# Segmented attention with a gated feed-forward block on one core: order of the first loads, warm-up operand, output buffers and the written order

## The chip, the cores and the metric

The kernel runs on one core of a Trainium2 chip. The metric is the device time of one execution in microseconds (us). TensorE (PE in the profile) multiplies matrices into PSUM, VectorE (DVE), ScalarE (ACT) and GpSimd (POOL) work on tiles, SyncE (SP) issues most DMAs and ScalarE some. Each engine runs its own instructions in the order in which they were written, and waits for the others on semaphores.

## The reference

All inputs are bf16. `x` is 2048 x 512; it is cut into 4 segments of 512 rows. Two branches read the same `x`, and a gate per row mixes them.

```
g   = sigmoid((x * gate_w).sum(-1))                      # one number a row
# branch a: 32 heads of width 16, 4 segments of 512 rows, in order
q, k, v = x @ wq, x @ wk, x @ wv
for s in range(4):
    a_dot = softmax(causal(q_s k_s^T / 4)) v_s
    a_mem = phi(q_s) M / (phi(q_s) z + 1e-6)             # phi(t) = t + 1 if t > 0 else exp(t)
    o_s   = sigmoid(beta) * a_mem + (1 - sigmoid(beta)) * a_dot
    M, z  = M + phi(k_s)^T v_s, z + phi(k_s).sum(rows)
a   = o @ wo
# branch b: feed-forward, width 1792
b   = (relu(x @ W_gate) * (x @ W_up)) @ W_down
out = g * a + (1 - g) * b
```

## The kernel before

The four segments are worked on one after another, and overlap. For a segment, TensorE projects q, k and v (`proj_q`, `proj_k`, `proj_v`), and for each group `c` of 8 heads it makes scores (`qk`, `qk_diag`), which ScalarE turns into exponentials `E` and `Em` (`score`), GpSimd and VectorE mask, and TensorE multiplies with the values (`pv`). VectorE divides by the row sums and turns the result into `oT` (`normalise`). From the second segment on, `dens` and `recall` add the memory's part by way of two DMAs through HBM (`coefs`, then `cdr`). `ffn_tasks` makes 14 feature tiles: a gate product, ScalarE's rectifier into `rgr`, an up product, and VectorE's product of both into `hT`. `out_tile` then adds `hT` times `wd_sb` and `oT` times `wo_sb` in one PSUM bank for 128 output rows. VectorE scales them by the row's factor (`ngcol`, L851) into a buffer of the ring `osr`, and SyncE stores that (L854). The ring has two buffers. The last 128 rows (tile 15) are made in two halves of 256 columns.

Matmuls come in three forms: whole (L442, all 128 x 128 of the array), cut into four strips of 32 columns (L446; also `pv`, `dens`, `memory`), and cut into four strips of 32 rows (the scores, L600 and L613). A projection, feed-forward or output matmul (a "flex" task) is issued whole or as four strips, according to what stands before it on TensorE.

**The order of the work is a written list.** Each piece of work is a `Task`, made by `plan.add` with an engine, a planned duration, the tasks it depends on, and the buffers it needs and frees. Tasks are numbered in the order of these calls. `ORDER` lists all 1337 numbers; `Plan.run` takes the tasks in that order, and each engine gets its instructions in it. `UNITS` gives, one hexadecimal digit a buffer, which buffer of its ring (or which of the 8 PSUM banks, `ps`) each piece of work uses. The planned durations and the landing times `LANDS` (in ns) don't act when the kernel runs; they are what the list was made from.

**The opening.** Loads are issued in program order. The first segment's `x` comes as four tiles of 128 rows into `xn` (names n0 to n3), and TensorE turns them with an identity matrix (`x0_tasks`, L478), VectorE and ScalarE copying the results to `xT` (L486; tile 1 and the second half of tile 3 on ScalarE). `wq` comes in two row halves (`load_q`), `wk` and `wv` whole. SyncE issues n0, the first half of wq, n3, the second half, wk, wv, then the gate and up weights in pieces; ScalarE issues n1 and n2. The first segment's q projection is split so that each half of `wq`, and the first two x tiles, can be used as they arrive (`proj_q`, `seg == 0`). Until the first tile is there, TensorE runs 6 matmuls on a tile of zeros (`heat`, L866), which VectorE sets first (`junk`, L312). Two more such matmuls of 256 columns (L493) are tasks of their own behind the turning of tiles 1 and 2; the list puts one of them there and the other, number 33, in the middle of the kernel.

Of the kernel before, what the change touches and what calls it, by code (L numbers as in the profile page):

```python
# [92 lines left out]
"""  # L93

UNITS = (
    "3527401612502452222115110640030222230110000031010000001001000000100100000320000137310d122a"
    "5222100c12292011023401083010111631250013103b1110000130311102301022221231212020224120112000"
    "0023001031000012001110000002300120320000120113137102a31122001020d1238123b01001035002920130"
    "106303c30240011110030201320210131200012021023332101062000002301112000003401012000000230111"
    "02100002301020320219211a203402200018120571271136302b320c21110233603d0000111130312130003112"  # L100
    "220312002002100000200111200000300110500000001011111000024000302032323029112b71332235714c21"
    "37720d3104602850665231522a1010010110"
)


class Slot:


    def __init__(self, cands):
        self.cands, self.units, self.left = tuple(cands), (), 0  # L110

    @property
# [66 lines left out]
def kernel(  # L179
# [64 lines left out]
    omr = ring([P, L], BF16, "omr", 3)  # L244
    dnr = ring([P, P], F32, "dnr", 2)
    cdr = ring([P, L], F32, "cdr", 2)
    osr = ring([P, D], BF16, "osr", 2)
    plan.pool("ps", 8)
    ps = psum.tile([P, 8 * L], F32, name="ps")

# [42 lines left out]
    def load_q(i):  # L293
        return load(nc.sync, wq_sb[:, 2 * i:2 * i + 2, :],
                    A_wq.rearrange("(c p) n -> p c n", p=P)[:, 2 * i:2 * i + 2, :], "q" + "ab"[i])
# [635 lines left out]
```

## Time and profile before

| what | value |
|---|---|
| median of 3 runs | 266.69 us (266.48, 266.69, 267.89) |
| profiled execution, its own time | 267.34 us |
| its span, first to last instruction | 265.5 us |
| busy in the span: PE, DVE, ACT, POOL | 260.6, 203.0, 183.0, 62.3 us |
| first matmul; first x tile turned; first q projection | 1.06, 3.59, 5.33 us |
| landings of n0, n1, first wq half, n2, n3, second wq half | 3.47, 3.64, 4.83, 4.87, 5.21, 5.92 us |
| landings of wk, wv, first gate piece, first up piece | 9.23, 10.74, 12.26, 13.74 us |
| last matmul ends; last scaling begins; last store lands | 261.69, 262.51, 264.56 us |
| DMA traffic | 19.43 MB, 73 GB/s in the mean, 340 to 380 GB/s from 3 to 14 us |

Times in the profile count from the first instruction. A line of the timeline has the start, the duration, the engine, the source line, the operation, the tiles written and read, the count, and in brackets how long the engine had been idle before and what ended that. Consecutive instructions of a kind are merged in it, and a matmul's end is modelled, so the distance between starts is the surer measure. PEld is the loading of a matmul's stationary operand. A landing is the last of the 16 parts into which a DMA is split.

### The profile page before, as it was taken

What the parts mean: (1) busy time and instruction counts of PE and PEld (TensorE: products, weight loads), DVE (VectorE), ACT (ScalarE), POOL (GpSimd) and SP (SyncE); (2) the same over time, 40 slices, a digit from 0 to 9 for tenths busy, and PEclk for the clock granted to TensorE, in tenths of its full rate; (3) what the DMA queues carried; (4) which work ended last, traced back from release to release, by engine and by line L of the source; (5) the groups of instructions that cost most, each with busy time, mean ns of one, the idle gap of its engine ahead of it and who ended that gap; (6) DMA issues with size and microseconds to landing.
All of it is one profiled execution on the core that took longest, in us unless ns stands there. A gap on an engine that the chain in (4) does not pass through costs nothing.

```text
span 265.5 us, 8410 instructions
## 1 busy us (share of the span) xinstructions
PE 260.6 (98%) x3646; PEld 120.2 (45%) x3646; DVE 203.0 (76%) x455; ACT 183.0 (69%) x168; POOL 62.3 (23%) x162
## 2 busy tenths in 40 slices
PE   8999999999999999999999999999999999999994
PEld 4543444453435444444443444444443544444553
DVE  3499698879897979899988988987882675476631
ACT  3098898979797798889889666889576663932000
POOL 7001914134114123141405140304004050210000
PEclk9999999999999999999999999999999999999999
DMA  6999916120002247610004231000300100300011
GB/s 222 347 217 345 295 37 87 34 71 2 2 30 46 91 75 116 165 32 2 2 12 62 81 85 49 16 2 1 129 6 0 42 0 7 124 3 0 2 42 42
DMA packets 29884, 19.43 MB, mean 73 GB/s; under 512 B 14872, under 2 KB 28312, under 8 KB 29848
## 3 DMA queue, kind: packets, MB, share of 16 engines
q1 hardware_dynamic: 29560, 18.64, 27.7%
q8 instruction: 28, 0.46, 0.8%
q10 hardware_dynamic: 288, 0.26, 0.3%
q14 instruction: 8, 0.07, 0.1%
HBM read 13.21 MB, written 2.55 MB: 59 GB/s over the span
## 4 chain that ended last, share of the span: by engine, by line
PE 95%; DMA 3%; DVE 0%; ACTq 0%; issue 0%; DVEq 0%
PE ps L442 63%; PE ps L446 14%; PE ps L600 8%; PE ps L673 7%; DMA out_dram<-osr 1%; DMA xn<-in_A_x_dram 1%; PE ps L613 1%; PE ps L778 1%; DVE osr L851 0%; PE ps L478 0%; PE ps L729 0%; ACTq L266 0%; PE ps L493 0%; DVEq L851 0%
## 5 line engine op out<-in xcount | busy, mean ns | idle before, releaser
L622 ACT ACTIVATE E<-ps 128x2048 bf16<-128x2048 f32 x64 | 120.1, 1877 | 31.9 <-PE ps L600 29.7
L651 POOL TENSOR_SCALAR_AFFINE_SELECT E<-E 128x256 bf16<-128x256 bf16 x128 | 53.5, 453 | 150.1 <-ACT E L622 150.0
L442 PE MATMUL ps<-xT,wu_sb 128*128 128x512 bf16 x200 | 54.4, 380 | 0.0
L829 DVE TENSOR_TENSOR hT<-ps,rgr 128x512 bf16<-128x512 f32 x56 | 38.2, 684 | 19.9 <-PE ps L442 14.2
L442 PE MATMUL ps<-xT,wg_sb 128*128 128x512 bf16 x188 | 49.5, 380 | 0.0
L823 ACT ACTIVATE rgr<-ps 128x512 bf16<-128x512 f32 x56 | 32.5, 596 | 15.5 <-PE ps L442 14.8
L442 PE MATMUL ps<-wd_sb,hT 128*128 128x512 bf16 x142 | 36.3, 380 | 0.0
L442 PEld LDWEIGHTS <-wu_sb 128*128 128x128 bf16 x200 | 18.2, 98 | 22.6 <-issue 3.0
L442 PEld LDWEIGHTS <-wg_sb 128*128 128x128 bf16 x188 | 17.7, 98 | 21.8 <-issue 1.7
L704 DVE STREAM_TRANSPOSE T<-ps 128x512 f32<-128x512 f32 x32 | 22.5, 709 | 5.0 <-PE ps L673 4.7
L600 PE MATMUL ps<-QT,KT 32*128 32x320 bf16 (+3 forms) x512 | 25.4, 273 | 0.0
L851 DVE TENSOR_SCALAR osr<-ps,ngcol 128x512 bf16<-128x512 f32 (+1 forms) x17 | 12.2, 717 | 12.1 <-PE ps L446 7.6
L446 PE MATMUL ps<-wd_sb,hT 128*32 128x512 bf16 (+1 forms) x384 | 21.2, 348 | 0.0
L442 PEld LDWEIGHTS <-hT 128*128 128x128 bf16 x142 | 13.1, 98 | 16.4 <-issue 2.1
L673 PE MATMUL ps<-E,Vp 128*17 128x320 bf16 (+3 forms) x512 | 19.4, 273 | 0.0
L600 PEld LDWEIGHTS <-KT 32*128 32x128 bf16 x512 | 7.6, 92 | 24.0 <-issue 23.1
L442 PE MATMUL ps<-xT,wk_sb 128*128 128x512 bf16 x64 | 18.1, 380 | 0.0
L622 ACT ACTIVATE Em<-ps 128x2048 bf16<-128x2048 f32 x8 | 15.0, 1878 | 4.1 <-PE ps L613 4.1
L442 PE MATMUL ps<-xT,wq_sb 128*128 128x512 bf16 (+1 forms) x64 | 15.9, 366 | 0.0
L549 DVE CAST ktr<-ps 128x512 bf16<-128x512 f32 x16 | 10.9, 684 | 3.4 <-PE ps L442 3.3
L764 DVE TENSOR_TENSOR omr<-ps,cdr 128x512 bf16<-128x512 f32 x12 | 8.1, 685 | 6.7 <-PE ps L442 6.3
L533 DVE CAST QT<-ps 128x512 bf16<-128x512 f32 x16 | 10.8, 680 | 2.9 <-PE ps L442 2.9
(97 smaller groups left out, 302.7 us busy)
## 6 DMA issues: line engine op xcount, KB each, us to landing
cdr<-coefs SPq DMA_DIRECT2D x12, 256.0 KB
out_dram<-osr SPq DMA_DIRECT2D x15, 128.0 KB
wd_sb<-in_B_W_down_dram SPq DMA_DIRECT2D x2, 896.0 KB
xn<-in_A_x_dram SPq DMA_DIRECT2D x3, 512.0 KB
wg_sb<-in_B_W_gate_dram SPq DMA_DIRECT2D x2, 512.0 KB
wu_sb<-in_B_W_up_dram SPq DMA_DIRECT2D x2, 512.0 KB
wg_sb<-in_B_W_gate_dram SPq DMA_DIRECT2D x2, 384.0 KB
wu_sb<-in_B_W_up_dram SPq DMA_DIRECT2D x2, 384.0 KB
```

The source lines that it names most:

```text
L442: nc.tensor.matmul(out, lhsT=lhsT, rhs=rhs, start=start, stop=stop)
L446: nc.tensor.matmul(out[r], lhsT=lhsT[:, r], rhs=rhs, start=start, stop=stop, tile_position=(0, 32 * j))
L533: prj["q", seg, c] = plan.add("DVE", 600, key - RQK, lambda: nc.vector.tensor_copy(QT[i][:], bank(sl)), [a], DVL, frees=[sl])
L549: d = plan.add("DVE", 600, key - RQK, lambda: nc.vector.tensor_copy(ktr[ks.i][:], bank(sl)), [a], DVL + 40, need=[ks], frees=[sl])
L600: nc.tensor.matmul(ps[:, j * L + o:j * L + o + L - q], lhsT=KT[i][rows, kb, 3 * r:3 * r + 2].rearrange("p h q -> p (h q)"), rhs=QT[i][rows ...
L622: last_exp[0] = [plan.add("ACT", 66 + 4 * L / 1.2, key, lambda: nc.scalar.activation(dst, ps[:, 0:4 * L], ACT.Exp, scale=SCALE), [a] + war ...
L651: nc.gpsimd.affine_select(out=m[:, :, o:o + HP], in_=m[:, :, o:o + HP], compare_op=ALU.is_ge, fill=0.0, base=HP, pattern=[[0, 4], [1, HP]] ...
L673: nc.tensor.matmul(bank(sl)[32 * j:32 * j + HW, q:q + w], lhsT=(Vp[i] if n < 4 else Vm)[:, kb, r, 4 * c + j, 0:HW], rhs=rhs, start=(n == 0 ...
L704: done.append(plan.add("DVE", 633, key - RL, lambda r=r, sl=sl: nc.vector.transpose(T[ts.i][:, r], bank(sl)), [a] + done, 75 if r else 0, ...
L823: r = plan.add("ACT", 478, key - RL, lambda sl=gsl, rs=rs: nc.scalar.activation(rgr[rs.i][:], bank(sl), ACT.Relu), [g], ACL, frees=[gsl])
L829: nc.vector.tensor_tensor(hT[hs1.i][:], bank(sl), rgr[rs.i][:], ALU.mult)),
L851: b = plan.add("DVE", 95 + 1.12 * w, key - RL, lambda: nc.vector.tensor_scalar(osr[os.i][:, 0:w], bank(sl)[:, 0:w], ngcol[:, tt:tt + 1], N ...
```

## The change

- The four x tiles are the first two DMAs of each queue: n0 and n2 on SyncE, n1 and n3 on ScalarE. Then come the two row halves of wq and, new, two row halves of wk, all on SyncE. `proj_k` waits for the half it reads.
- The warm-up reads a constant 1.0 that the program's preamble sets, in place of the zeroed tile, and has 7 matmuls: 6 of 512 columns and one of 256.
- One of the two L493 matmuls is left out.
- `osr` has three buffers.
- `LANDS`, the planned time of the Vm copy (480 in place of 680) and the size of the warm-up in the plan are changed, and `ORDER` and `UNITS` are new throughout.

```diff
-    osr = ring([P, D], BF16, "osr", 2)
+    osr = ring([P, D], BF16, "osr", 3)
...
-    LANDS = dict(n0=3500, n1=3600, n2=4850, qa=5000, n3=5500, qb=6350, k=8600, v=10100, g0=11600,
+    LANDS = dict(n0=3650, n1=3800, n2=4650, n3=4800, qa=5350, qb=6350, ka=7700, kb=8900, v=10300,
...
-    def load_q(i):
-        return load(nc.sync, wq_sb[:, 2 * i:2 * i + 2, :],
-                    A_wq.rearrange("(c p) n -> p c n", p=P)[:, 2 * i:2 * i + 2, :], "q" + "ab"[i])
-
-    got_n[0] = [load_x0(nc.sync, 0)] + [load_x0(nc.scalar, t) for t in (1, 2)]
-    got_q = [load_q(0)]
-    got_n[0].append(load_x0(nc.sync, 3))
-    got_q.append(load_q(1))
-    got_k = load_cols(nc.sync, wk_sb, A_wk, 0, D, "k")
+    def load_rows(t, ap, i, name):
+        return load(nc.sync, t[:, 2 * i:2 * i + 2, :],
+                    ap.rearrange("(c p) n -> p c n", p=P)[:, 2 * i:2 * i + 2, :], name + "ab"[i])
+
+    got_n[0] = [load_x0(nc.scalar if t % 2 else nc.sync, t) for t in range(4)]
+    got_q = [load_rows(wq_sb, A_wq, i, "q") for i in range(2)]
+    got_k = [load_rows(wk_sb, A_wk, i, "k") for i in range(2)]
...
-            if n in (1, 2):
+            if n == 1:
...
-        a = matmuls(key, [got_k] + war, sl, proj_mm(wk_sb, c, seg),
-                    chunk={ci: got_x[seg][ci // 2] for ci in range(NC)})
+        a = matmuls(key, war, sl, proj_mm(wk_sb, c, seg),
+                    chunk={ci: got_x[seg][ci // 2] + [got_k[ci // 2]] for ci in range(NC)})
...
-        att["vm", seg] = [plan.add("DVE", 680, K(4 * seg - 2 - (1 if seg else 0), 2000), lambda r=r: (
+        att["vm", seg] = [plan.add("DVE", 480, K(4 * seg - 2 - (1 if seg else 0), 2000), lambda r=r: (
...
-        for k in range(6):
-            nc.tensor.matmul(bank(warm[k % 8]), lhsT=junk[:, 0:P],
-                             rhs=junk[:, None, 0:P].to_broadcast([P, 4, P]), start=True,
-                             stop=True)
-    plan.add("PE", 3500, -1e9, heat, lat=0, need=warm, frees=warm, size=12)
+        one = nc.const_aps.tensor(1.0, (P, 1), BF16)
+        for k in range(7):
+            w = L if k < 6 else L // 2
+            nc.tensor.matmul(bank(warm[k])[:, 0:w], lhsT=one.to_broadcast([P, P]),
+                             rhs=one.to_broadcast([P, w]), start=True, stop=True)
+    plan.add("PE", 3500, -1e9, heat, lat=0, need=warm, frees=warm, size=14)
```

In the new list's last rows, the ring `osr` is used as follows: tile 13 buffer 0, tile 14 buffer 2, tile 12 buffer 0, tile 15's first half buffer 2, its second half buffer 1. In the old one: 0, 1, 0, 1 and 0.

More of the change, by code (lines that the diff above doesn't have):

```diff
@@ L30 @@
 ORDER = """
[62 rows of a table removed]
[61 rows of a table added]
 """
 UNITS = (
[L96 to L102, printed above, removed]
+    "54231670213504642013512210203720122021000002000000003301100000310000000023001602d021b01363"
+    "119122a00143121002512372202323320302238113c10010210021102112200111011002110110221300120000"
+    "0230011210000320011100000020011302000000301122152030203b22033129322d30023126301c110a120122"
+    "083134302701121001213211221120123003301211233121301310000023011010000023011012000003101021"
+    "31000032010010a222d303010271108023401120245203c123330210026113b313901120110123022322031027"
+    "02202203103100000220101200000200001520000021001011000035011705022283033124501740022013b311"
+    "d321a2226306c5129724131371010020211"
 )
@@ L255, in work @@
         return plan.one("ps", range(7, -1, -1))
-    LANDS = dict(n0=3500, n1=3600, n2=4850, qa=5000, n3=5500, qb=6350, k=8600, v=10100, g0=11600,
-                 u0=13000, gw=13500, be=13700, g1=15100, u1=16550, x1=19800, g2=21700, u2=22900,
-                 g3=24000, u3=25150, d0=28050, d1=30600, o=32000)
+    LANDS = dict(n0=3650, n1=3800, n2=4650, n3=4800, qa=5350, qb=6350, ka=7700, kb=8900, v=10300,
+                 g0=11700, u0=13100, gw=13500, be=13700, g1=15100, u1=16550, x1=19800, g2=21700,
+                 u2=22900, g3=24000, u3=25150, d0=28050, d1=30600, o=32000)
     def arrival(name):
```

123 rows, old and new, of the table ORDER are left out of this document.

## The prediction

> **What bounds the kernel now.** I read the page first (busy shares, then the chain that ended last), then the timeline of the first 16 us, the chain of the last 40 us and the timeline of the last 8 us, and last the groups of ScalarE and VectorE.
>
> ```profile
> PE 260.6 (98%) x3646; PEld 120.2 (45%) x3646; DVE 203.0 (76%) x455; ACT 183.0 (69%) x168; POOL 62.3 (23%) x162
> PE 95%; DMA 3%; DVE 0%; ACTq 0%; issue 0%; DVEq 0%
> ```
>
> TensorE is the chain for 95% of the span. Busy shares of a pipelined engine can flatter, so I looked at the distance from one matmul's start to the next: from 7 us on it is 0.216 us for every 512 columns, whether the matmul is whole (L442) or cut into four column strips (L446: 17 such groups fill 247.88 to 251.54, 0.215 each). Only 0.36 us in all is lost to waits there: 0.12 before the first wv matmul, and two misses of 0.12 near 130 us. So the middle has nothing to give but its own work. What is left are the two ends.
>
> ```profile
> 1.06 2.74 PE L866 MATMUL ps<-junk 128*128 128x512 bf16 x6 [1.06 <-DVE mcol_e L326]
> 3.59 1.06 PE L478 MATMUL ps<-ident,xn 128*128 128x128 bf16 x8
> 4.45 0.42 PE L493 MATMUL ps<-junk 128*128 128x256 bf16 x1
> 4.92 0.61 PE L478 MATMUL ps<-ident,xn 128*128 128x128 bf16 x4
> 5.33 0.63 PE L442 MATMUL ps<-xT,wq_sb 128*128 128x256 bf16 x2
> ...
> 9.28 1.06 PEld L442 LDWEIGHTS <-wk_sb 128*128 128x128 bf16 x6 [0.23 <-DMA wk_sb<-in_A_wk_dram]
> 9.37 1.46 PE L442 MATMUL ps<-xT,wk_sb 128*128 128x512 bf16 x6
> 10.78 0.11 PEld L442 LDWEIGHTS <-xT 128*128 128x128 bf16 x2 [0.45 <-DMA wv_sb<-in_A_wv_dram]
> ```
>
> Columns: start, duration, engine, line, operation, tiles, count, idle time before. Six 512-column matmuls take 2.74 us at 1.06 and 1.46 us at 9.37: the opening runs at half pace (0.427 against 0.216). Start by start, the half pace holds until 6.81; the page's clock row shows nothing of it. The last lines show wk and wv arriving just as they are needed.
>
> ```profile
> 258.59 3.80 DMA out_dram<-osr
> ```
>
> ```profile
> 260.86 0.83 PE L446 MATMUL ps<-wo_sb,oT 128*32 128x256 bf16 x24
> 261.31 0.48 DVE L851 TENSOR_SCALAR osr<-ps,ngcol 128x256 bf16<-128x256 f32 x1 [2.74 <-PE ps L446]
> 262.51 0.48 DVE L851 TENSOR_SCALAR osr<-ps,ngcol 128x256 bf16<-128x256 f32 x1 [0.72 <-DMA out_dram<-osr]
> ```
>
> TensorE is done at 261.69, but the last scaling starts at 262.51. It writes the buffer that the store issued at 258.59 still reads, and that store took 3.80 us. The stores before and after it took 1.73 and 1.53. In the packet records one 16 KB instruction packet runs from 259.64 for 1.58 us; fifteen of the store's sixteen parts had landed by 260.29, one at 262.39.
>
> **The change part by part.** The sum is made against the profiled execution: 267.34 us, a span of 265.5 and 1.8 around it. It lies 0.65 above the median of the three runs (266.69).
>
> *Third osr buffer.* In the new written order the last half tile writes buffer 1, whose earlier store (tile 10) is queued before the stores of the last four tiles; buffers 0 and 2 serve the others. The last scaling then starts when TensorE ends: 262.51 - 261.69 = 0.82 saved. Behind it scaling (0.48), store (1.54) and closing steps stay. What is late next is TensorE itself. Bounds: 0.82, and 0.1 if the slow store is this execution's own: at 1.7 us it would not be waited for, and only the place behind the first half (261.79) would be gained. I take 0.82: the instruction stream is the same in every run.
>
> *Warm-up on a constant.* The first matmul waits for VectorE's memsets (0.89 to 1.01). The constant is written by 0.48, and the engines are let go at 0.74 to 0.80 (first DMA issue 0.80), so it can start near 0.83. Six and a half matmuls of 0.427 end at 3.62 instead of 3.59: +0.03. If the full pace also comes 0.2 us sooner, half of that is saved. [...]
>
> *Four x tiles first.* Now tile 2 lands at 4.87 beside half of wq (384 KB in 1.23 us behind the first pair), and TensorE idles 0.26 us (4.66 to 4.92). With tiles 2 and 3 alone the second pair is 256 KB: 0.82 us, an estimate from that row, so 4.47, as the flips of tiles 0 and 1 end (3.62 + 8 x 0.107 = 4.48). Tile 2, half of tile 3 and the filler follow to 5.33. The first wq half, now third, comes 0.82 later, 5.3; the ScalarE copy of tile 1, which ended at 5.28, binds as well. By 6.81 the old order had done 5 of the 256-column wq matmuls; the new one does (6.81 - 5.33 - 0.21 for the rest of tile 3) / 0.213 = 5.9. Saved 0.9 x 0.109 = 0.1. Bounds 0 and 0.26/2 = 0.13. The tile that moves queue takes a slot of 0.43 us on SyncE and frees one on ScalarE, where nothing waits before 4.69. [...]
>
> *wk in halves.* One more issue on SyncE, 0.47 us, ahead of wv, the gate weights and all later loads; the transfers are the limit there (wk, wv, first gate and up pieces land at 9.23, 10.74, 12.26, 13.74: 1.5 us apart), so they move little. In the new order four more 512-column matmuls stand before the first wv one: its 0.12 us wait goes. But the first gate matmul comes 2.6 us sooner in matmul time, and falls at about 12.4 against 12.26: free, with no margin. The third gate piece (landed 21.41, now about 21.9) is first used near 22.5. I take -0.12; bounds -0.12 and +0.2.
>
> *Filler.* The second one ran uselessly at 131.88 and cost 0.12; gone.
>
> *Written order.* Each number in the list is a task in the order of the plan.add calls, so it can be counted. TensorE changes between whole, row-strip and column-strip matmuls 145 times before, 146 after; a change costs 0.095 (0.312 from a whole matmul to a score instead of 0.216): +0.1. Matmuls cut in four: 208 before, 177 after, free by the pace above. Between two scores stand at least 10 matmuls (2.16 us) after, 2.08 us before. A bank is reused, or a product read, no sooner than 5 matmuls (1.08 us) after its own last matmul in either list, and before shows that this suffices but for two misses. So I take 0, with 0.25 better (both misses gone) and 1 us worse (eight more) as bounds. The plan's shorter time for the Vm copy (480 for 680) moves nothing by itself; the copies take 0.454.
>
> Sum: -0.82 - 0.07 - 0.1 - 0.12 - 0.12 + 0.1 = -1.13, to 266.2 for such an execution. Part of the profiled opening, wv's 0.12, may be absent in a median run, so there I count -1.05: 266.69 - 1.05 = 265.6.
>
> **The rivals.**
>
> *Earlier full pace.* The half pace lasted 5.75 us from the first matmul here. If the earlier start and the missing idle bring the release to where the wq matmuls begin (5.33), the 1.48 us up to 6.81 shrink by half, 0.74. Against it: the gate weights at 12.26 leave only 0.2 of that in an execution like this one; the spread of the runs (1.4 us) says that such openings vary. I take 0.6: 265.0. [...] Chance 0.20.
>
> *The slow store is the profiled execution's own.* Then the third buffer changes little, and 265.6 + 0.7 = 266.3. For it: the profiled execution is 0.65 above the median, almost this wait. Against it: the same instructions are fetched in every run. Chance 0.15.
>
> *Slower: ScalarE's list becomes the bound.*
>
> ```profile
> L622 ACT ACTIVATE E<-ps 128x2048 bf16<-128x2048 f32 x64 | 120.1, 1877 | 31.9 <-PE ps L600 29.7
> L823 ACT ACTIVATE rgr<-ps 128x512 bf16<-128x512 f32 x56 | 32.5, 596 | 15.5 <-PE ps L442 14.8
> ```
>
> A score waits for the exponential before it, and ScalarE works in order. Between exponentials 492 and 495 the new list puts a Vp copy (754), a rectifier (560) and a phi exponential (698): 1.88 + 0.58 + 0.60 + 0.63 = 3.7 us, where TensorE's list has 2.59 between the scores. At 1124 and 805 three more stand as well: excesses 1.1, 0.85 and 0.7, where the old list's worst is 0.65. Each next distance is wide (3.7, 3.7, 3.45 against 2.59), which absorbs them. It decides against the change where the rectifier's product is itself next on TensorE: then the excess is paid, at most 2.65 in all: 268.2. Pairs with ScalarE the longer are fewer after (14) than before (16), and before none shows a stall. Chance 0.12.
>
> **How the numbers follow.** My forecast has 0.53, its own range 265.0 to 266.4. A measurement of this kernel can tell about 0.5%, 1.33 us: faster is below 265.36, slower above 268.02. Faster: 0.18 of the forecast's 0.53, and 0.19 of the first rival: 0.37. Slower: 0.11 of the last. Same: 0.52. The range runs from 264.4 (the earlier release at its full 0.74, both misses gone, and the better bounds of the opening) to 267.5 (no gain at the end, the 1 us bound of the new order and the 0.2 of the gate weights), and leaves out most of the last rival.
>
> **What would show it.** Right: first matmul near 0.83; no idle between 4.5 and 5.3; wv and gate weights without a wait over 0.15; no filler near 131; the last scaling released by TensorE, with starts still 0.216 apart between. Wrong: scores spaced wider than 10 matmuls need, ScalarE named as releaser of TensorE; or a store or instruction packet that lands on the very last store, which would add up to 3.80 - 1.53 = 2.3 us.

## The result and the profile after

The changed kernel took 266.43 us (median of 16 runs, 265.49 to 266.96) beside 267.07 for the kernel before (16 runs, 266.21 to 268.19): 0.64 us less, ratio 0.9969 with a 95% interval of 0.9954 to 0.9984. That is within the 0.5% that the prediction called no change. In a later comparison of the same two kernels (a_again, below) it was 266.50 beside 266.66, ratio 0.9997 (0.9982 to 1.0012). So the gain is 0.64 and 0.16 us by the medians, 0.8 and 0.1 by the ratios, and the second comparison cannot tell it from nothing. Medians and ranges here are of all runs; the ratios leave out a run that is over 1.5% above the fastest of its kernel. They are not quotients of the medians: where a few late runs weigh, the two differ, and the interval decides.

The profiled execution took 266.44 us with a span of 264.7 (before: 267.34 and 265.5). From the page of the changed kernel, the busy times and the engines of the chain that ended last:

```profile
PE 257.0 (97%) x3520; PEld 119.1 (45%) x3553; DVE 200.7 (76%) x455; ACT 182.8 (69%) x168; POOL 62.4 (24%) x162
PE 91%; DVE 3%; ACT 2%; issue 2%; DMA 2%; SPq 0%; ACTq 0%
```

TensorE is still the chain. Its lower count is partly a matter of records: 33 matmuls of this execution are not in the trace (3520 against 3553 weight loads), so the 3.6 us less of busy time are no gain. The gaps that they leave, most of them 0.22 us, the time of one matmul, stand as "issue" in the chain and lower TensorE's share of it. The first stretch, TensorE's lines of the timeline of the changed kernel (start, duration, then as before):

```profile
0.84 2.93 PE L865 MATMUL ps<-const-bfloat16-1.0 128*128 128x512 bf16 x7 [0.84 <-PEq L913]
3.66 1.67 PE L475 MATMUL ps<-ident,xn 128*128 128x128 bf16 x14
5.12 0.42 PE L490 MATMUL ps<-junk 128*128 128x256 bf16 x1
5.95 0.66 PE L439 MATMUL ps<-xT,wq_sb 128*128 128x256 bf16 x4 [0.41 <-DMA wq_sb<-in_A_wq_dram]
...
8.30 1.03 PE L439 MATMUL ps<-xT,wk_sb 128*128 128x512 bf16 x4
...
11.32 1.03 PE L439 MATMUL ps<-wv_sb,xT 128*128 128x512 bf16 x4
12.18 0.60 PE L439 MATMUL ps<-xT,wg_sb 128*128 128x512 bf16 x2
```

The warm-up starts at 0.84 and no longer waits for VectorE, the wv and gate weights are met without a wait, and there is a new wait: the first wq matmul starts at 5.95, released by the DMA of wq's first half, which landed at 5.91 (before: 4.83). The filler at 5.12 ends its 0.213 us of half pace at 5.34, so TensorE stood still for 0.61 us (the bracket says 0.41, since the modelled end runs on; all standstills below are read from the starts in this way). With 0.09 us ahead of the first x tile that makes 0.70 of standstill at half pace. Half pace ended at 6.06 (before 6.95, read in the same way inside the one matmul that has both paces; the prediction's 6.81 is that matmul's start).

The end, VectorE's lines of the timeline:

```profile
259.59 0.48 DVE L848 TENSOR_SCALAR osr<-ps,ngcol 128x256 bf16<-128x256 f32 x1 [1.00 <-PE ps L443]
261.34 0.48 DVE L848 TENSOR_SCALAR osr<-ps,ngcol 128x256 bf16<-128x256 f32 x1 [1.26 <-PE ps L443]
```

The last scaling is now released by TensorE, at 261.34 in place of 262.51. TensorE's last matmul ends at 261.29 (before 261.69). Of these 1.17 us the span keeps 0.81: a 16 KB instruction packet ran from 261.13 for 1.43 us. One of the 16 parts of the store issued at 260.10 landed at 263.64, the others by 261.63; and the last store (issued 261.85) landed its last part at 263.82, the others by 263.38: 0.44 lost.

### The profile page after: what moved, and what is told of

Same layout as the page of the kernel before. It is cut to its first block, busy times and chain, and to the rows that moved or that the text cites. A ratio compares the mean times of both kernels' runs of the same rounds, so it can differ in the third digit from the quotient of the medians.

```text
span 264.7 us, 8203 instructions
## 1 busy us (share of the span) xinstructions
PE 257.0 (97%) x3520; PEld 119.1 (45%) x3553; DVE 200.7 (76%) x455; ACT 182.8 (69%) x168; POOL 62.4 (24%) x162
## 4 chain that ended last, share of the span: by engine, by line
PE 91%; DVE 3%; ACT 2%; issue 2%; DMA 2%; SPq 0%; ACTq 0%
PE ps L439 63%; PE ps L443 12%; PE ps L597 7%; PE ps L670 7%; DMA wq_sb<-in_A_wq_dram 2%; ACT E L619 1%; PE ps L610 1%; DVE T L701 1%; DVE osr L848 0%; ACT rgr L820 0%; PE ps L726 0%; SPq L265 0%; DVE hT L826 0%; DVE och L706 0%; PE ps L775 0%
## 5 line engine op out<-in xcount | busy, mean ns | idle before, releaser
L439 PE MATMUL ps<-xT,wg_sb 128*128 128x512 bf16 x184 | 50.4, 380 | 0.3 <-issue 0.2
L439 PE MATMUL ps<-wd_sb,hT 128*128 128x512 bf16 x145 | 39.7, 380 | 1.1 <-issue 1.0
L439 PEld LDWEIGHTS <-wu_sb 128*128 128x128 bf16 x206 | 19.0, 98 | 23.4 <-issue 2.5
L439 PEld LDWEIGHTS <-hT 128*128 128x128 bf16 x154 | 14.0, 98 | 17.6 <-issue 2.5
L439 PE MATMUL ps<-xT,wq_sb 128*128 128x512 bf16 (+1 forms) x71 | 17.9, 356 | 0.6 <-DMA wq_sb<-in_A_wq_dram 0.4
L443 PE MATMUL ps<-wd_sb,hT 128*32 128x512 bf16 (+1 forms) x336 | 17.9, 344 | 0.0
L439 PE MATMUL ps<-xT,wk_sb 128*128 128x512 bf16 x59 | 15.9, 380 | 0.2 <-issue 0.2
L439 PE MATMUL ps<-wv_sb,xT 128*128 128x512 bf16 x52 | 14.7, 380 | 0.1
```

What stands on the lines that cost most here:

```text
L439: nc.tensor.matmul(out, lhsT=lhsT, rhs=rhs, start=start, stop=stop)
L443: nc.tensor.matmul(out[r], lhsT=lhsT[:, r], rhs=rhs, start=start, stop=stop, tile_position=(0, 32 * j))
```

## The experiments

Theory at the start: the third buffer pays what it showed (0.82 us), and the packet at 261.13 takes 0.4 of it back. Rivals: the slow store is a chance of one execution, or the new written order costs something that hides the gain. The kernels from a_again on follow a theory that came out of the first four: that a standstill of TensorE in the opening, a time in which it has no matmul to run, prolongs half pace (a_more_instr: 1.17 us of it, half pace until 9.75). The kernels were run in four groups on three chips, each group beside the kernel before; kernels of different groups are compared by way of it.

**The third buffer alone** (b_third_buffer, the kernel before with)

```
-    osr = ring([P, D], BF16, "osr", 2)
+    osr = ring([P, D], BF16, "osr", 3)
 # UNITS: the last half tile's digit 0 -> 2
```

> The kernel before, with a third osr buffer used by the last half tile alone; nothing else. Theory (the wait of 0.72 us for the slow store of tile 12 is there in every run and is the third buffer's whole worth): the last scaling is released by TensorE at about 261.7 of the span instead of 262.51, the store of tile 12 still takes about 3.8 us, and the time falls by 0.8 us (ratio 0.997). Rival (the slow store was the one profiled execution's own): the store takes 1.7 us, the last scaling moves by at most 0.1, ratio 1.000.

266.41 us beside 266.93 (12 and 35 runs), ratio 0.9987 (0.9969 to 1.0005); span 264.8. VectorE's last line of its timeline:

```profile
261.29 0.92 DVE L851 TENSOR_SCALAR osr<-ps,ngcol 128x256 bf16<-128x256 f32 x2 [2.75 <-PE ps L446]
```

Both scalings now run in one go (x2, two of 0.48 back to back); before, the second stood apart and waited for the store. The store was as slow as before: the packet ran at 259.44, and the part that it held up landed at 262.03, the other fifteen by 260.27. TensorE ends at 261.67, as before; the last store is issued at 262.24 in place of 263.02. So the slow store belongs to the instruction stream, and the buffer saves 0.78 in the trace and 0.52 by the medians, though the interval still includes no change.

**The packet moved** (b_more_instr: the kernel before; a_more_instr: the changed one; 30 matmuls of segment 4 as four column strips each)

```
+STRIPS = {...}  # numbers of the tasks
...
-                t.col = bool(t.flex) and mode == "col"
-                mode = mode if t.col else t.mode
+                t.col = bool(t.flex) and (mode == "col" or t.n in STRIPS)
+                mode = "col" if t.col else t.mode
```

> The kernel before, two osr buffers, but 30 matmuls of the fourth segment issued as four column strips (180 more TensorE instructions, same pace, same number of mode changes), so that TensorE's last 16 KB instruction fetch comes about 2.4 us earlier, at 257.2 instead of 259.64. Theory (that fetch makes tile 12's store slow): the store of tile 12 takes 1.7 us, the wait for it is gone without a third buffer, and the time falls by 0.7 to 0.8 us (ratio 0.997). Rival (something else slows that store): store 3.8 us, last scaling at 262.5, ratio 1.000.

266.39 beside 266.93, ratio 0.9984 (0.997 to 0.9999). The last packet was expected at 257.2 and came at 259.98, so it moved, but the other way: the store issued at 258.36 had landed whole by 260.07, before the packet could hold it up. With two buffers and the same last tiles, the wait is gone. VectorE's last line:

```profile
261.07 0.92 DVE L853 TENSOR_SCALAR osr<-ps,ngcol 128x256 bf16<-128x256 f32 x2 [2.74 <-PE ps L448]
```

The wait of 0.82 can thus be removed by a buffer or by moving the packet; each gives about 0.5 by the medians. The interval of the first includes no change, that of the second barely leaves it out.

> The changed kernel, with 30 matmuls of the fourth segment issued as four column strips (180 more TensorE instructions), so that the last instruction fetch comes about 2.4 us earlier, at about 258.7 instead of 261.13, ahead of the last two stores. Theory (that fetch delays a part of the last two stores, which cost the changed kernel 0.43 us of its gain): both last stores land 1.55 us after their issue, the last at 263.4 instead of 263.8, and the time is 0.4 us below the changed kernel's, ratio to before 0.995. Rival (the late part has another cause): last landing 2.0 us after its issue as now, time as the changed kernel's, ratio 0.997.

266.54 beside 266.93, ratio 0.9998 (0.9974 to 1.0021), but the profiled execution took 268.15, and two more of the 12 runs 268.33; the other nine lie between 266.04 and 266.98. Its end was clean: packet at 260.72 (not at 258.7, as expected), last store landed in 1.53 us. The ratio of 0.995 that was expected did not come. The 2 us of the late runs are, in the one that was profiled, in the opening. TensorE's lines of its timeline:

```profile
5.06 0.42 PE L492 MATMUL ps<-junk 128*128 128x256 bf16 x1
6.44 1.04 PE L441 MATMUL ps<-xT,wq_sb 128*128 128x256 bf16 x4 [0.96 <-DMA wq_sb<-in_A_wq_dram]
7.27 0.42 PE L477 MATMUL ps<-ident,xn 128*128 128x128 bf16 x2
7.49 3.02 PE L441 MATMUL ps<-xT,wq_sb 128*128 128x256 bf16 x14
10.34 1.03 PE L441 MATMUL ps<-xT,wk_sb 128*128 128x512 bf16 x4
```

Here wq's first half landed at 6.40 and TensorE stood still from 5.28 to 6.44. Behind that it worked on at half pace: the fourteen wq matmuls take 3.02 us, in the profile of the changed kernel 1.91. Half pace ended at 9.75. This was not expected by any theory, and became the next question.

**Two buffers for the last four tiles** (a_two_at_end, the changed kernel with)

```
-    "d321a2226306c5129724131371010020211"
+    "d321a2226306c5129724131371010010110"
```

> The changed kernel, with the last four tiles on two osr buffers in turn as before (0, 1, 0, 1, 0). Theory (two buffers cost something only where an instruction fetch meets the store that is waited for; here the fetch of 261.1 comes after tile 12's store of 258.6 has landed at 260.3): the last scaling is still released by TensorE, and the time is that of the changed kernel within 0.1 us. Rival (the third buffer itself is worth 0.8): the last scaling waits for a store, 0.8 us slower than the changed kernel, ratio to before about 1.000.

266.81 beside 266.93, ratio 1.0006 (0.999 to 1.0023). In its trace the last scaling is released by TensorE even so, and every part of the last stores landed in time: the packets fell at 256.86 and 265.01.

```profile
261.54 0.48 DVE L848 TENSOR_SCALAR osr<-ps,ngcol 128x256 bf16<-128x256 f32 x1 [1.26 <-PE ps L443]
```

By these traces two buffers suffice in the new order. With them the last scaling waits for tile 12's store alone. That store landed ahead of TensorE's last matmul in all ten traces of the new order, by 0.37 to 0.97 us; in the changed kernel's own it landed at 260.32, and TensorE ended at 261.29. The median does not settle the buffer's worth: the two comparisons of the unaltered kernel differ by as much.

**The changed kernel again** (a_again)

> The changed kernel unaltered, for its spread. Theory of the standstill: TensorE stands still from about 5.3 us until the first half of wq lands (5.9 to 6.4 us in the three profiles with this opening). [...] Then a few of the 12 runs, 0 to 4, should lie at 267.8 to 268.4 and the others at 265.5 to 267. Theory of bytes: wq's first half is late by its own 0.6 us and nothing else; no run over 267.5, one group.

266.50 beside 266.66; 265.76 to 267.73, and only the last over 267.1. In its profile wq's first half landed at 6.82:

```profile
4.72 0.27 PE L490 MATMUL ps<-junk 128*128 128x256 bf16 x1
6.86 0.61 PE L439 MATMUL ps<-xT,wq_sb 128*128 128x256 bf16 x4 [1.86 <-DMA wq_sb<-in_A_wq_dram]
```

The filler takes 0.11 us at full pace, so TensorE stood still for 2.03 us. But half pace had already ended at 4.35, and full pace stayed. This suggests that a standstill costs itself and, if it falls ahead of the release (the end of half pace), more: the matmuls ended at 262.16 here, and at 263.35 in a_more_instr with 1.17 us of it ahead of the release. One run over 267.5 in twelve does not decide between the two theories; the next pair does.

**A later wq, without and with filler** (a_late_wq, a_late_wq_filled: the changed kernel with)

```
-    got_q = [load_rows(wq_sb, A_wq, i, "q") for i in range(2)]
-    got_k = [load_rows(wk_sb, A_wk, i, "k") for i in range(2)]
...
+    rows(wk_sb, A_wk, 0)
+    rows(wq_sb, A_wq, 0)
+    rows(wq_sb, A_wq, 1)
+    rows(wk_sb, A_wk, 1)
...
 # and in the second one, the filler's matmul (L490) nine times in place of once
```

> The changed kernel with wk's first half sent ahead of both halves of wq, so that the first wq matmul waits until about 6.6 to 7.2 us and TensorE stands still for 1.3 to 1.9 us. Theory of the standstill: a third to two thirds of the runs keep half pace until about 9.5 us; they form a group 1.4 to 1.9 us above the rest, and the median goes up by 0.6 to 2 us. Theory of bytes: one group, all of it 0.4 to 0.8 us above the changed kernel.

> The same late wq, with the filler issued nine times (1.7 us more at half pace, to about 7.0 us), so that TensorE stays busy while it waits. Theory of the standstill: no second group; half pace ends between 4.5 and 7 us, and all runs lie 0.3 to 0.8 us above the changed kernel, below the median of the unfilled one. Theory of bytes: like the unfilled one or up to 0.3 us above it.

Unfilled: 267.62 beside 266.66, ratio 1.004 (1.0013 to 1.0067). The 12 runs spread over 266.31 to 267.80 (seven), 268.54 to 268.69 (three) and 270.15, 270.49. Filled: 266.81, all 12 between 266.37 and 267.45, ratio 1.0001 (0.9985 to 1.0018). The loads are the same in both. The filler does no work that counts, and takes 0.8 us off the median; of the runs over 267.5 it leaves none, where there were six. TensorE's lines of both timelines, unfilled first:

```profile
5.07 0.42 PE L498 MATMUL ps<-junk 128*128 128x256 bf16 x1
7.59 1.03 PE L447 MATMUL ps<-xT,wq_sb 128*128 128x256 bf16 x4 [2.09 <-DMA wq_sb<-in_A_wq_dram]
8.41 0.42 PE L483 MATMUL ps<-ident,xn 128*128 128x128 bf16 x2
8.63 3.62 PE L447 MATMUL ps<-xT,wq_sb 128*128 128x256 bf16 x14
12.04 1.69 PE L447 MATMUL ps<-xT,wk_sb 128*128 128x512 bf16 x4
```

```profile
5.13 1.87 PE L498 MATMUL ps<-junk 128*128 128x256 bf16 x9
6.87 0.61 PE L447 MATMUL ps<-xT,wq_sb 128*128 128x256 bf16 x4
7.32 0.27 PE L483 MATMUL ps<-ident,xn 128*128 128x128 bf16 x2
7.43 1.91 PE L447 MATMUL ps<-xT,wq_sb 128*128 128x256 bf16 x14
```

Unfilled (the run of 270.49), TensorE stood still from 5.28 to 7.59 and kept half pace until 13.37; filled, half pace ended at 6.61, among the nine fillers, and the same fourteen matmuls took 1.91. The unfilled execution ended its matmuls 3.54 us later than the filled one (265.70 against 262.16). The groups of the unfilled runs lie about 1.7 us apart (268.6 and 270.3; five of the seven lowest between 266.3 and 267.1). By an estimate from that distance and the two paces (0.427 and 0.216 us for 512 columns), each group would have kept half pace for about 3.4 us more than the one below it; only the run of 270.49 was profiled.

**The filler in the changed kernel** (a_filled)

```
-                plan.add("PE", 213, K(-9) + n + 0.5, lambda js=js: nc.tensor.matmul(
+                plan.add("PE", 213, K(-9) + n + 0.5, lambda js=js: [nc.tensor.matmul(
...
+                    for _ in range(5)], [a],
```

> The changed kernel with the filler between tile 3 and the first wq matmul issued five times in place of once: 0.85 us more of work at half pace, to 6.2 us. Theory of the standstill: TensorE never stands still for over 0.3 us, half pace ends between 4.5 and 7 us in every run, no run over 267.5; the median is 0 to 0.3 us below the changed kernel's. Theory of bytes: the filler only delays wq's matmuls by the 0.2 us that it outlasts the landing in most runs: median 0.1 to 0.2 above the changed kernel's, spread as it was.

266.46 beside 266.66, ratio 1.0001 (0.9988 to 1.0014), 265.87 to 267.32. Against a_again (266.50) the median is the same, so in the changed kernel as it stands the standstill's price does not show in the medians. No standstill was left in its trace; half pace ended at 5.87, and the first wq matmul came at 5.94.

**The old order of the loads** (a_old_tiles, a_old_tiles_more with the 180 added instructions, a_old_tiles_filled with those and three fillers ahead of the turning of tile 3)

```
-    got_n[0] = [load_x0(nc.scalar if t % 2 else nc.sync, t) for t in range(4)]
-    got_q = [load_rows(wq_sb, A_wq, i, "q") for i in range(2)]
...
+    tile0(nc.sync, 0)
+    tile0(nc.scalar, 1)
+    tile0(nc.scalar, 2)
+    qrows(0)
+    tile0(nc.sync, 3)
+    qrows(1)
...
 # a_old_tiles_filled, ahead of the first matmul that turns tile 3:
+                for _ in range(3 if (t, c0) == (3, 0) else 0):
+                    nc.tensor.matmul(bank(sl)[:, 2 * P:4 * P], lhsT=junk[:, 0:P],
+                                     rhs=junk[:, None, 0:P].to_broadcast([P, 2, P]),
+                                     start=True, stop=True)
```

> The changed kernel with the opening loads in the order of the kernel before: tile 0 on SyncE, tiles 1 and 2 on ScalarE, first half of wq, tile 3, second half of wq; wk still in halves. Theory of the late wq: wq's first half lands near 4.9 and tile 3 near 5.2, the standstill shrinks from 0.6 to 1.9 us to about 0.3 us, wk's first matmul starts at 7.7 to 8.5 us, and the median lies 0.2 to 0.7 us below the changed kernel's on the same chip (ratio to before 0.996 to 0.999). Theory of the prediction (tiles first saves 0.1): median 0.1 us above the changed kernel's.

266.61 beside 266.75, ratio 1.0 (0.9979 to 1.0021), two of 12 runs at 267.88 and 268.30. wq's first half landed at 4.91, but now tile 3, at 5.29, is what TensorE stands still for (0.48 us); its first wq matmul came at 5.73. The trace ends its matmuls 0.28 earlier than the changed kernel's (261.01), the runs do not: which of the two loads comes late matters little. Neither theory's number came: the kernel lies 0.14 below the kernel before, the changed kernel in its own comparison 0.16.

> The same old order of the opening loads in the changed kernel, with 30 matmuls of segment 4 written as four column strips each, which adds 180 TensorE instructions and puts the last 16 KB instruction packet elsewhere than beside the last two stores. If that packet costs the changed kernel 0.4 us at the end, as its trace reads, the median lies 0.2 to 0.4 us below that of the old tile order alone; if the packet is fetched at another place in most runs, the two agree within 0.15.

266.29, 0.32 below the same without the added instructions, though the intervals cannot tell the two apart (ratio 1.0001, 0.9978 to 1.0023); three of 12 runs at 267.84 to 268.13. In its trace the packet came at 258.49 and the last store landed in 1.54 us.

> The kernel with the old order of opening loads and the 180 added TensorE instructions, with three more filler matmuls (0.64 us at half pace) ahead of tile 3's flips, where TensorE stood still for 0.5 us. Theory of the standstill: half pace ends between 4.3 and 7 us, no run over 267.5 (without the filler 3 of 12 lay at 267.8 to 268.1), median 265.9 to 266.3, ratio to before 0.997 to 0.9985. Theory that the late runs have another cause: 2 to 3 of 12 stay above 267.8 and the median does not move.

265.99 beside 267.05 (7 and 12 runs), ratio 0.9961 (0.9946 to 0.9976); all seven between 265.62 and 266.19. TensorE's lines of its timeline:

```profile
4.55 0.49 PE L490 MATMUL ps<-junk 128*128 128x256 bf16 x3
5.81 0.28 PE L494 MATMUL ps<-ident,xn 128*128 128x128 bf16 x2 [0.77 <-DMA xn<-in_A_x_dram]
```

In this execution half pace had ended before the fillers (by 3.98, where 4.3 to 7 was expected), so the trace does not show them at work. The late runs of the two kernels above it (5 of 24) are absent from the seven, but seven runs are too few to call them gone. It has the lowest median of all kernels run, and beats the kernel before; against the changed kernel (0.9969 and 0.9997) the intervals overlap.

**Two parts on the kernel before** (b_warm_third: the edit of b_third_buffer, and)

```
-        for k in range(6):
-            nc.tensor.matmul(bank(warm[k % 8]), lhsT=junk[:, 0:P],
...
+        one = nc.const_aps.tensor(1.0, (P, 1), BF16)
+        for k in range(7):
+            w = L if k < 6 else L // 2
+            nc.tensor.matmul(bank(warm[k])[:, 0:w], lhsT=one.to_broadcast([P, P]),
...
```

> The kernel before with two parts of the change only: the warm-up on the constant and the third buffer for output rows (the last half tile writes buffer 2). Prediction's terms: 0.82 and 0.07 us saved, median 0.9 below before. Theory that the third buffer is worth about 0.5 by the median and an earlier start only draws among the releases of half pace: 0.4 to 0.7 below before, ratio 0.9975 to 0.9985.

266.21 beside 266.75, ratio 0.9992 (0.9973 to 1.0012). The buffer alone gave 0.52, so the earlier start (0.84) added nothing that can be seen. Its profiled execution is its slowest run, 268.22, and the one case of a long standstill with the old loads:

```profile
4.42 0.42 PE L493 MATMUL ps<-junk 128*128 128x256 bf16 x1
5.71 0.60 PE L478 MATMUL ps<-ident,xn 128*128 128x128 bf16 x4 [0.86 <-DMA xn<-in_A_x_dram]
...
6.96 4.07 PE L442 MATMUL ps<-xT,wq_sb 128*128 128x256 bf16 x20
10.87 1.46 PE L442 MATMUL ps<-xT,wk_sb 128*128 128x512 bf16 x5
```

Tile 2 landed at 5.66, TensorE stood still for 1.07 us, and half pace went on until 9.18. It ended its matmuls at 263.40, 1.73 behind b_third_buffer.

**All openings together.** Half pace's end is interpolated from the distances between starts; the standstill is the part of it that fell before that end.

| kernel profiled | first matmul | standstill | half pace ends | last matmul ends |
|---|---|---|---|---|
| b_third_buffer | 1.05 | none | 4.01 | 261.67 |
| b_more_instr | 1.06 | none | 4.02 | 261.46 |
| a_old_tiles_filled | 0.84 | 0.25 | 3.98 | 261.35 |
| a_again | 0.84 | none | 4.35 | 262.16 |
| a_two_at_end | 0.84 | 0.12 | 4.68 | 261.48 |
| a_old_tiles | 0.84 | 0.48 | 5.72 | 261.01 |
| a_old_tiles_more | 0.84 | 0.50 | 5.87 | 261.11 |
| a_filled | 0.84 | none | 5.87 | 261.24 |
| after | 0.84 | 0.70 | 6.06 | 261.29 |
| a_late_wq_filled | 0.84 | 0.10 | 6.61 | 262.16 |
| before | 1.06 | 0.26 | 6.95 | 261.69 |
| b_warm_third | 0.84 | 1.07 | 9.18 | 263.40 |
| a_more_instr | 0.84 | 1.17 | 9.75 | 263.35 |
| a_late_wq | 0.84 | 2.34 | 13.37 | 265.70 |

With a standstill of up to 0.70 us, half pace ends 3.0 to 5.9 us after the first matmul; with 1.07 and more, 8.3 to 12.5 us after it. What ends half pace, no trace shows. Over the runs: of the three kernels with more filler, none of 31 lies over 267.5; of the six with the changed kernel's opening or the old loads and no added filler (after, a_again, a_two_at_end, a_more_instr, a_old_tiles, a_old_tiles_more) 11 of 76. Kernels and chips are mixed in these counts; the pair a_late_wq and a_late_wq_filled, six of twelve against none, is the clean comparison.

## Why the prediction was right, and where its steps were not

The forecast (265.6 in its range of 264.4 to 267.5, no change the likeliest) held, but the gain was 0.64 and 0.16 where 1.05 was summed, and 266.43 lies just above the forecast's own 265.0 to 266.4. That the range held says little for the sum, since it spans 3.1 us, and the number nearest to the result, 266.3, belongs to a rival whose mechanism fell. Part of the miss in the time is the base: the kernel before had a median of 266.69 over three runs, and 267.07 over 16. Between the two profiled executions the span fell by 0.81 us. TensorE's last matmul ended 0.40 earlier, where the terms other than the buffer's sum to 0.31, and 0.41 were saved behind it, where the buffer's term had 0.82. Step by step:

- **Third buffer, 0.82.** On the old order the mechanism was right: last scaling released by TensorE, the slow store in the instruction stream (in all three traces of the old order without added instructions). The rival that called it the execution's own fell. By size the term was too large: 0.78 in the trace, 0.52 by the medians of the buffer alone. In the changed kernel the wait went as forecast, but by luck and not by the buffer: the packet no longer met tile 12's store, and by the traces two buffers would have done (a_two_at_end). Instead the packet met the last two stores, the step that the prediction named as what would make it wrong; it cost 0.44, against the 2.3 named as the most. The same happens in a_again, a_filled, a_late_wq_filled and a_old_tiles: the packet starts between 0.33 us before the last matmul's end and 0.05 behind it, and the last store's last part lands 0.15 to 0.43 behind the others. By the medians this price does not show (a_more_instr, a_old_tiles_more).
- **Warm-up, 0.07.** Start at 0.84 as foretold. An earlier end of half pace that comes from it cannot be told from the 2.9 us over which that end varies; by the medians nothing. No run shows that full pace comes 0.2 us sooner with the earlier start, as the term had it: half pace ended at 9.18 with a start at 0.84 (b_warm_third, 1.07 of standstill) and at 4.01 with one at 1.05 (b_third_buffer).
- **Four tiles first, 0.10.** The mis-sized term. It took 5.3 for wq's first half; the five traces with these loads show 5.89 to 6.82. The idle time at tile 2 went, and a longer one came at wq. The step had none there, since its 5.3 met the filler's end at 5.33. It also counted standstill at its own length alone, whereas with 1.07 us of it ahead of the release (b_warm_third) half pace went on until 9.18 and the matmuls ended 1.73 us behind b_third_buffer's, and with 1.17 (a_more_instr) until 9.75 and 2.06 behind the changed kernel's, where it was 0.70 and 6.06. That rival side, a late load that prolongs half pace, was not among the three. By the medians the term is worth nothing that can be seen: with the old order of these loads (a_old_tiles) the time is the same.
- **wk in halves, 0.12.** Right: wk, wv and gate weights without a wait; the first gate piece had landed at 11.52, ahead of the 12.26 that left no margin; the first gate matmul came at 12.18.
- **Filler, 0.12.** Right as to its absence; its worth was not measured by itself.
- **Written order, +0.1.** Waits of TensorE from 13 us on that are not changes of form add up to 0.31 us before and 0.25 after, as far as the records go. ScalarE did not become the bound. An estimate from the starts: the time from the end of half pace to the last matmul, and the full-pace time of the work done before it (fillers left out), come to 256.25 us before and 256.06 after; 0.24 of the difference are wv's wait and the filler of the kernel before, so the new order costs about 0.05.
- **The earlier full pace (rival, 0.20)** came in part in the profiled execution (6.06 for 6.95, where it had 5.33); when half pace ends differs from execution to execution (6.06 and 4.35 in the two of the unaltered changed kernel). Its worth is limited by the loads, as the prediction said of the gate weights: b_third_buffer had full pace from 4.01 and ended its matmuls at 261.67, the kernel before from 6.95 and at 261.69. In between it waited for wk:

```profile
9.15 1.47 PE L442 MATMUL ps<-xT,wk_sb 128*128 128x512 bf16 x5 [0.39 <-DMA wk_sb<-in_A_wk_dram]
```

What stays open: how much of the gain that is missing in the medians is the packet at the end and how much the opening, since each price shows in traces alone; how much of the difference between 0.64 and 0.16 is the openings of these runs and how much the kernel before, whose median moved between 266.66 and 267.07 from one comparison to the next; and what sets the place of the last instruction packet, which in a_two_at_end, with the same matmuls, lay 4 us behind that of the changed kernel.

## What to carry to other kernels

In this kernel TensorE started at half pace, and a wait in the first microseconds had two prices: its own length, and, in the three profiles in which 1.07 us or more of it fell before half pace ended, half pace until 9.18 to 13.37 in place of 3.98 to 6.95. Filler matmuls that outlast the landing of the next operand took the second away (a_late_wq has six of 12 runs over 267.5, a_late_wq_filled none), and cost nothing that shows in the changed kernel (266.46 in a_filled, 266.50 in a_again). A wait that goes away with a change need not have gone by the part that was meant to remove it: put that part back alone and look. A gain at the very end has to be read in the last store's slowest part (here 263.82, the others by 263.38), not in the last compute instruction. A change worth 0.3% needs its parts read in the trace and its runs as a distribution: here the medians differed less than the tails.

## What the runs showed of the hardware

- Half pace of TensorE ended 3.0 to 5.9 us after the first matmul in eleven profiles, 8.3 to 12.5 us after it in the three with a standstill of 1.07 us or more ahead of it. A standstill of 2.03 us after the end (a_again) did not bring half pace back: the fourteen wq matmuls behind it took 1.91 us, as in the changed kernel's profile, and 3.02 where half pace went on until 9.75 (a_more_instr). The clock row of the page shows none of this: in the pages of before and after it is a 9 in every slice.
- Where a 16 KB instruction packet (0.9 to 1.6 us) started 0.03 to 1.23 us behind a store's issue, one of the store's 16 parts came late, and the scaling that waited for the store in the kernel before started only behind that part (262.51, the part at 262.39). How late the part came went with how far into the store the packet started: 0.4 and 0.6 us behind the others for 0.03 and 0.05 us behind the store's issue, 1.4 to 1.5 for 0.45 and 0.69, 1.7 to 2.1 for 0.85 to 1.23 (262.39 against 260.29 before; 263.64 against 261.63 after), and nothing from 1.49 on (in b_more_instr 1.62). A packet that started ahead of the issue and still ran cost 0.1 to 0.4 (0.44 after). With 180 more TensorE instructions it came at 259.98 in place of 259.64 (b_more_instr) and at 260.72 in place of 261.13 (a_more_instr), and neither tile 12's store in the first (whole by 260.07) nor the last store in the second (landed in 1.53 us) had a late part.
- wq's first half, third on its queue, landed 5.89 to 6.82 us after the start in five executions with one and the same order of issues (issued at 1.73 to 1.75).
